# The product of the carried state with q, in a turned mLSTM chunk, on four quarters of the PE array in place of two

## The chip, the cores and the metric

The kernel runs on one core of a Trainium2 chip. The metric is the device time of one execution in microseconds (us); for a kernel it is the median of several executions. A profile of one further execution is read beside it. Engines are named as the profile names them: PE is TensorE's matmuls, PEld its weight loads, DVE is VectorE, ACT is ScalarE, POOL is GpSimd, SP issues the DMAs.

## The reference, cut to what matters

An mLSTM cell runs over 768 steps for 4 batches of 8 heads with 40 dimensions each; its output, seen as 3072 tokens of 320 values, goes through a feed-forward layer with a squared ReLU.

```python
def _attn_ref(q, k, v, i_gate, f_gate, o_gate):          # q, k, v, o_gate: (4, 8, 768, 40)
    ...
    for t in range(S):
        ...                                              # f_stab, i_stab: gates, stabilised
        C = f_stab[:, :, None, None] * C + i_stab[:, :, None, None] * np.einsum('bhd,bhe->bhde', vt, kt)
        n = f_stab[:, :, None] * n + i_stab[:, :, None] * kt
        h_tilde = np.einsum('bhde,bhe->bhd', C, qt)
        nq = np.einsum('bhd,bhd->bh', n, qt)[:, :, None]
        denom = np.maximum(np.abs(nq), 1.0)
        o = 1.0 / (1.0 + np.exp(-o_gate[:, :, t]))
        y[:, :, t] = o * h_tilde / denom
    return y

def _moe_ref(x, w_in, w_out):                            # x: (3072, 320); w_in: (320, 2048)
    h = np.maximum(x @ w_in, 0.0)
    return h * h @ w_out
```

The kernel does not step through time. It cuts the sequence into chunks of 128 steps: 4 batches of 6 chunks, s = 0 to 23, with c = s mod 6 the place in the batch. Within a chunk the output is a masked product (q k), weighted, times v; what came before the chunk enters as q times the state C that the chunk before left. At c = 0 there is no such state. C carries n as its 41st column, so a head gives 41 numbers for each step: 40 of the numerator and the denominator.

## The kernel before: the parts concerned

Chunks 0 to 5 take an older path. From chunk 6 on a chunk is "turned": its numerator stands with the 41 values of a head on partitions and the 128 steps along the row. With W = 512, P = 128, PR = 4, DP = 64, D = 40, D1 = 41:

```python
    ps_at = ctx.enter_context(tc.tile_pool(name="ps_at", bufs=3, space=PSUM))      # three PSUM banks
    ...
    def scores(s, o=(False, False)):              # L420: k q of a chunk, two banks of the pool
        d = st[s]
        sc = [bank(o[i]) for i in range(2)]       # bank(): ps_at.tile([P, W], F32, name="tp", tag="at")
        for j in range(PR):
            for i in range(2):
                rows = slice(DP * i, DP * i + D)
                nc.tensor.matmul(
                    sc[i][:, j, :], lhsT=d["kT"][rows, j, :], rhs=d["qT"][rows, j, :], start=True, stop=True,
                )
        d["sc"] = sc

    def weighted(s, spare=False):                 # L433: VectorE reads the two banks, writes P[0], P[1]
        ...
        for i in range(2):
            ...
            nc.vector.tensor_tensor(t, d["sc"][i], d["W"][:, heads, :], op=ALU.mult)

    def attend_turned(s):
        b, c = divmod(s, NB)
        d = st[s]
        halves = [slice(DP * i, DP * (i + 1)) for i in range(2)]
        live = [slice(DP * i, DP * i + D) for i in range(2)]
        numT = ps_at.tile([P, PR, P], F32, name="numT", tag="at")

        if c > 0:
            C = C_b[(s - 1) % 2]
            for j in range(PR):
                for i in range(2):                # L503: 40 rows and 64 columns of the array each
                    nc.tensor.matmul(
                        numT[halves[i], j, :], lhsT=C[live[i], j * D1 : j * D1 + DP], rhs=d["eA"][live[i], j, :],
                        start=(j == 0), stop=False, skip_group_check=True,
                    )
        for j in range(PR):
            for i in range(2):                    # L510: 128 rows, 64 columns
                h = PR * i + j
                nc.tensor.matmul(
                    numT[halves[i], j, :], lhsT=va_w[s % NKQ][:, h * D1 : h * D1 + DP],
                    rhs=d["P"][h % 2][:, h // 2, :] if s < KQ_SQ else d["P"][i][:, j, :],
                    start=(c == 0 and j == 0), stop=True, skip_group_check=True,
                )
        if c + 1 < NB:
            dC = ps_at.tile([P, PR, D1], F32, name="dC", tag="at")
            ...                                   # L520: eight matmuls, 128 rows, 40 columns: k v of the chunk

        tn = attn.tile([P, P // SQ, PR, SQ], F32, name="tn", bufs=1)
        nc.vector.transpose(tn[:].rearrange("p m j r -> p j m r"), numT[:].rearrange("p j t -> p (j t)"))   # L525
        d["tn"] = tn
        if c + 1 < NB:
            ...                                   # L531: the new C from dC and the decayed old one
```

The eight heads lie as h = 4 i + j: i picks the half of the array's rows in which a head's 40 dimensions of q and C stand (partitions 0 to 39 or 64 to 103). Before the change the same i also picks the half of the columns, and so of numT's partitions. `tn` goes out to DRAM and comes back with steps on partitions (N); `normalise_turned` divides by the denominator and multiplies by the output gate.

The order of work: a chunk takes four slots, each holding one part of the feed-forward of earlier tokens. Slot 0 is `score` (scores and weighted), then a part; slot 1 is `attend_turned`, then a part, and so on. A part is made of full-array matmuls: L625 and L636 (x w_in), L719 (h w_out, in seven products).

```python
        if at == 0:
            do(score, s)
        if at == 1:
            do(attend_turned, s)
            do(decays, s + 1)
            do(mask, s + 1)
            ...
        if which == 1:
            ffn1_main(g, i)
            ...
        elif g == 0:
            ffn2(g, *divmod(i, 2))
        else:
            ffn2_fast(g, i)
        if at == 2:
            ...
            do(normalise_turned, s)
```

Of the kernel before, what the change touches and what calls it, by code (L numbers as in the profile page):

```python
# [9 lines left out]
F32 = mybir.dt.float32  # L10
# [7 lines left out]
P = 128  # L18
# [11 lines left out]
def kernel(  # L30
# [27 lines left out]
    nc = tc.nc  # L58
    B, H, S, D = q.shape
# [3 lines left out]
    PR = H // 2  # L63
    DP = 64
    D1 = D + 1
    DM = H * D
# [5 lines left out]
    W = 4 * P  # L72
# [9 lines left out]
    ps_at = ctx.enter_context(tc.tile_pool(name="ps_at", bufs=3, space=PSUM))  # L82
# [16 lines left out]
    NKQ = 4  # L99
    kq_b = [consts.tile([P, 2, H, DP], F32, name=f"kq{i}") for i in range(NKQ)]  # L100

    va_w = [consts.tile([P, H * D1 + 24], F32, name=f"va{i}") for i in range(NKQ)]
# [177 lines left out]
    KQ_SQ, X_SQ = 7, 6  # L280
# [209 lines left out]

    def attend_turned(s):

        b, c = divmod(s, NB)
        d = st[s]
        halves = [slice(DP * i, DP * (i + 1)) for i in range(2)]
        live = [slice(DP * i, DP * i + D) for i in range(2)]
        numT = ps_at.tile([P, PR, P], F32, name="numT", tag="at")

        if c > 0:
            C = C_b[(s - 1) % 2]  # L500
            for j in range(PR):
                for i in range(2):
                    nc.tensor.matmul(  # L503
                        numT[halves[i], j, :], lhsT=C[live[i], j * D1 : j * D1 + DP], rhs=d["eA"][live[i], j, :],
                        start=(j == 0), stop=False, skip_group_check=True,
                    )
        for j in range(PR):
            for i in range(2):
                h = PR * i + j
                nc.tensor.matmul(  # L510
                    numT[halves[i], j, :], lhsT=va_w[s % NKQ][:, h * D1 : h * D1 + DP],
                    rhs=d["P"][h % 2][:, h // 2, :] if s < KQ_SQ else d["P"][i][:, j, :],
                    start=(c == 0 and j == 0), stop=True, skip_group_check=True,
                )
        if c + 1 < NB:
            dC = ps_at.tile([P, PR, D1], F32, name="dC", tag="at")
            for j in range(PR):
# [3 lines that stand above are left out]
                        dC[live[i], j, :], lhsT=d["kq"][:, 0, h, :D], rhs=d["vw"][:, h, :], start=True, stop=True,  # L521
                    )

        tn = attn.tile([P, P // SQ, PR, SQ], F32, name="tn", bufs=1)
        nc.vector.transpose(tn[:].rearrange("p m j r -> p j m r"), numT[:].rearrange("p j t -> p (j t)"))  # L525
        d["tn"] = tn
        if c + 1 < NB:
            Cn = C_b[s % 2][:, : PR * D1].rearrange("p (j d) -> p j d", d=D1)
            for rows in live:
                if c > 0:  # L530
                    nc.vector.tensor_tensor(Cn[rows], dC[rows], d["Cd"][rows], op=ALU.add)  # L531
                else:
                    nc.vector.tensor_copy(Cn[rows], dC[rows])
# [13 lines left out]
    def normalise_turned(s):  # L547
        d = st[s]
        N = d["N"].rearrange("p (g e j r) -> p g e j r", g=2, e=2, r=SQ)
        R = D - SQ  # L550
        den = N[:, :, 1, :, R]
        dm = work.tile([P, H], F32, name="dm")
        dm2 = dm[:].rearrange("p (g j) -> p g j", g=2)
        nc.vector.tensor_scalar(dm2, den, scalar1=-1.0, scalar2=1.0, op0=ALU.mult, op1=ALU.max)
        nc.vector.tensor_tensor(dm2, dm2, den, op=ALU.max)
        nc.vector.reciprocal(dm[:], dm[:])
        x = d["x"] = work.tile([P, 3 * P], F32, name="x_sb")
        x3 = x[:, :DM].rearrange("p (h d) -> p h d", d=D)
        x4, og = x[:, :DM].rearrange("p (g j d) -> p g j d", g=2, d=D), d["og"].rearrange("p (g j) d -> p g j d", g=2)
        nc.vector.tensor_tensor(x4[:, :, :, :SQ], N[:, :, 0], og[:, :, :, :SQ], op=ALU.mult)  # L560
        nc.vector.tensor_tensor(x4[:, :, :, SQ:], N[:, :, 1, :, :R], og[:, :, :, SQ:], op=ALU.mult)
        nc.vector.tensor_tensor(x3, x3, dm[:].unsqueeze(2).to_broadcast([P, H, D]), op=ALU.mult)
        nc.vector.tensor_copy(x[:, DM:], x[:, DM - KR : DM])
# [290 lines left out]
    for u in range(8):  # L854
        s = 2 + u // 2
# [72 lines left out]
    for n, (which, g, i) in enumerate(parts):  # L928
        s, at = 6 + n // 4, n % 4
# [5 lines left out]
# [4 lines that stand above are left out]
            if n > 4:  # L939
                do(turn_kq, s + 1)  # L940
            do(decay_C, s + 1)
            if s > X_SQ:
                do(turn_squares, s - 1)
            do(store_num, s)
            do(load, s + 4)
            if 8 <= s < 20:
                load_o(s + 4)
            do(load_num, s)
            do(pair_up, s + 3)
# [37 lines left out]
        if at == 2:  # L987
            do(lambda s: weigh(s, masked=True), s + 1)
            if n < 4:
                do(turn_kq, s + 1)  # L990
                do(scale_q, s + 1)
            do(normalise_turned, s)
            do(store_rows, s)
            do(load_squares, s + 2)
            do(load_rows, s)
            do(load_A, s + 2)
# [33 lines left out]
```

## Time and profile before

| what | value |
|---|---|
| median of 3 executions | 533.74 us (531.35 to 535.14) |
| span of the profiled execution | 534.1 us |
| mean granted PE clock | 0.986 |
| L503, q C | x240 matmul records, mean 275 ns |
| L510, P v | x288, mean 279 ns |
| L525, transpose of numT | x18, mean 717 ns |

In the profile each fp32 matmul of the program shows as two records of PE and two of PEld: the 8 matmuls of L503 in a chunk are 16 records, and 15 chunks with c > 0 make the 240. A record's duration is not the time that the matmul costs: records overlap, so the cost of a group is read from where it starts and where the next group starts. In a line of a timeline the columns are start in us, length in us, engine, line, operation, output and inputs, shape, and the number of records merged; a bracket tells of idle time before it. The shape `40*64` of a matmul is rows times columns of the array in use, `40x128` the moving operand.

### The profile page before, as it was taken

The page shows a single profiled execution, that of the slowest core. Times are in us where ns is not written, and L with a number is a line of the kernel's source. Part 1 is how long each engine was busy: PE and PEld are TensorE (multiplying, and loading weights), DVE is VectorE, ACT ScalarE, POOL GpSimd, SP SyncE. Part 2 cuts the span into 40 slices and gives each one's busy share as a digit, 9 for nine tenths or more (in the row PEclk, how much of TensorE's full clock was granted, in tenths as well). Part 3 has the DMA queues.
Part 4 walks back from the last instruction along what each step waited for, and adds up shares of the span by engine and source line. Part 5 has one row for each costly group of instructions (what it writes and reads, how often), then busy time and mean ns, then how long its engine had stood idle before and what let it go on. Part 6 is the DMA issues. An engine that isn't in the chain of part 4 may idle for free.

```text
span 534.1 us, 10320 instructions
## 1 busy us (share of the span) xinstructions
PE 523.7 (98%) x3928; PEld 457.7 (86%) x3929; DVE 328.5 (62%) x620; ACT 194.6 (36%) x460; POOL 91.4 (17%) x110
## 2 busy tenths in 40 slices
PE   8999989998999999999999999999999999999997
PEld 4878878886798898898898898898898898998997
DVE  8488988958874764654764754664764764532531
ACT  3766577552441422522422623313632413102100
POOL 3255633331320210110210200100210200000000
PEclk9897999998999999999999999999999999999999
DMA  9998699877576587585686576677566162110000
GB/s 193 224 197 179 162 159 203 193 180 157 109 155 116 119 161 139 116 168 116 134 170 130 114 153 111 154 150 135 131 137 127 55 128 49 53 42 2 26 25 26
DMA packets 239394, 68.06 MB, mean 127 GB/s; under 512 B 185744, under 2 KB 233872, under 8 KB 239344
## 3 DMA queue, kind: packets, MB, share of 16 engines
q1 hardware_dynamic: 239248, 67.20, 60.2%
q8 instruction: 31, 0.51, 0.4%
q10 hardware_dynamic: 96, 0.20, 0.1%
q14 instruction: 19, 0.16, 0.1%
HBM read 55.08 MB, written 17.86 MB: 137 GB/s over the span
## 4 chain that ended last, share of the span: by engine, by line
PE 85%; DVE 6%; ACT 3%; DMA 3%; SPq 2%; issue 1%; POOL 0%; DVEq 0%; POOLq 0%; ACTq 0%
PE h_ps L719 32%; PE h_ps L625 27%; PE h_ps L636 7%; PE tp L420 4%; PE numT L510 3%; PE h_ps L665 3%; PE numT L503 3%; PE hp L456 1%; DVE g L658 1%; DMA num_rows<-tn 1%; ACT W_sb L382 1%; SPq L308 1%; PE tp L408 1%; PE dC L520 1%; DMA kq<-in_q_dram 1%
## 5 line engine op out<-in xcount | busy, mean ns | idle before, releaser
L625 PE MATMUL h_ps<-xT,w_in 128*128 128x256 f32 x768 | 175.1, 384 | 0.6 <-ACT xT L610 0.6
L625 PEld LDWEIGHTS h_ps<-xT,w_in 128*128 128x128 f32 x768 | 143.8, 191 | 22.0 <-issue 1.2
L658 DVE TENSOR_TENSOR g<-r_sb 128x512 f32<-128x512 f32 x96 | 61.7, 701 | 67.0 <-ACT r_sb L651 67.0
L651 ACT ACTIVATE r_sb<-h_ps 128x512 f32<-128x512 f32 x96 | 49.9, 600 | 115.8 <-PE h_ps L636 112.7
L719 PE MATMUL h_ps<-w_out,g 128*128 128x160 f32 x528 | 77.0, 302 | 0.0
L719 PEld LDWEIGHTS h_ps<-w_out,g 128*128 128x128 f32 x528 | 72.5, 190 | 1.4
L358 POOL TENSOR_SCALAR_AFFINE_SELECT A_bc<-A_bc 128x1024 f32<-128x1024 f32 x22 | 26.2, 1192 | 216.8 <-ACT kq L368 183.0
L382 ACT ACTIVATE W_sb<-A_bc,b_T 128x128 f32<-128x128 f32 x176 | 53.8, 391 | 13.4 <-POOL A_bc L358 13.3
L719 PE MATMUL h_ps<-T,S 128*128 128x160 f32 x352 | 52.3, 302 | 0.0
L719 PEld LDWEIGHTS h_ps<-T,S 128*128 128x128 f32 x352 | 48.8, 190 | 3.0 <-ACT r_sb L651 3.0
L368 ACT ACTIVATE kq<-A_bc 64x512 f32<-64x512 f32 x30 | 18.8, 628 | 83.3 <-DMA A_bc<-a_rows 83.1
L636 PE MATMUL h_ps<-xT,w_in 64*128 64x256 f32 x384 | 49.0, 391 | 0.0
L636 PEld LDWEIGHTS h_ps<-xT,w_in 64*128 64x128 f32 x384 | 34.8, 186 | 12.3 <-issue 9.0
L525 DVE STREAM_TRANSPOSE tn<-numT 128x512 f32<-128x512 f32 x18 | 12.9, 717 | 36.2 <-PE numT L510 36.1
L433 DVE TENSOR_TENSOR P_sb<-tp,W_sb 128x512 f32<-128x512 f32 x46 | 29.5, 682 | 4.4 <-PE tp L420 4.4
L735 DVE TENSOR_TENSOR y_sb<-y_sb,h_ps 128x160 f32<-128x160 f32 x44 | 14.1, 320 | 26.4 <-PE h_ps L719 25.8
L394 POOL TENSOR_TENSOR vw<-va,W_sb 128x328 f32<-128x328 f32 x20 | 18.3, 916 | 67.4 <-ACT W_sb L382 60.6
L739 ACT COPY y_sb<-h_ps 128x160 f32<-128x160 f32 x11 | 3.2, 293 | 66.3 <-PE h_ps L719 66.3
L420 PEld LDWEIGHTS tp<-kqT 40*128 40x128 f32 x384 | 24.2, 187 | 3.3 <-issue 2.3
L420 PE MATMUL tp<-kqT 40*128 40x128 f32 x384 | 26.9, 279 | 0.0
L719 PE MATMUL h_ps<-T,g 128*128 128x160 f32 x176 | 25.7, 299 | 0.0
L719 PE MATMUL h_ps<-w_out,S 128*128 128x160 f32 x176 | 25.7, 299 | 0.0
(119 smaller groups left out, 610.6 us busy)
## 6 DMA issues: line engine op xcount, KB each, us to landing
A_bc<-a_rows SPq DMA_DIRECT2D x23, 512.0 KB, 5.0
raw<-in_moe_w_out_dram SPq DMA_DIRECT2D x16, 320.0 KB, 3.4
num_rows<-tn SPq DMA_DIRECT2D x18, 256.0 KB, 3.0
kq<-num_rows SPq DMA_DIRECT2D x72, 64.0 KB, 2.5
kqT<-kq_rows SPq DMA_DIRECT2D x34, 128.0 KB, 3.3
raw<-in_moe_w_in_dram SPq DMA_DIRECT2D x8, 512.0 KB, 4.7
kq<-in_k_dram SPq DMA_DIRECT2D x24, 160.0 KB, 4.4
va<-in_v_dram SPq DMA_DIRECT2D x24, 160.0 KB, 4.6
```

Of the source, the lines that this page charges most:

```text
L358: nc.gpsimd.affine_select(A[:], A[:], compare_op=ALU.is_ge, fill=-1e30, base=0, pattern=[[0, H], [1, P]], channel_multiplier=-1,)
L368: nc.scalar.activation(e[rows], st[s]["A"][0][rows, PR * i : PR * (i + 1), :], AF.Exp)
L382: nc.scalar.activation(d["W"][:, i * n + h, :], A[i][:, h, :], AF.Exp, bias=b_T[:, b, c, i * n + h : i * n + h + 1],)
L394: nc.gpsimd.tensor_tensor(d["vw"][:], d["va"][:], d["W"][:, :, P - 1 : P].to_broadcast([P, H, D1]), op=ALU.mult,)
L420: nc.tensor.matmul(sc[i][:, j, :], lhsT=d["kT"][rows, j, :], rhs=d["qT"][rows, j, :], start=True, stop=True,)
L433: nc.vector.tensor_tensor(t, d["sc"][i], d["W"][:, heads, :], op=ALU.mult)
L503: nc.tensor.matmul(numT[halves[i], j, :], lhsT=C[live[i], j * D1 : j * D1 + DP], rhs=d["eA"][live[i], j, :], start=(j == 0), stop=False, s ...
L625: nc.tensor.matmul(hs[i][:, n, :], lhsT=w_in[:, a, fb * P : (fb + 1) * P], rhs=xT[:, :, a, :], start=(n == 0 and a == 0), stop=False,)
L636: nc.tensor.matmul(hs[i][:, n, :], lhsT=w_in2[rows, 2 * pp + n, :], rhs=xT[rows, :, 2, :], start=False, stop=(n == 1),)
L651: nc.scalar.activation(rs[-1][:], h[:], AF.Relu)
L658: nc.vector.tensor_tensor(g4[:, :, i, :], r[:], r[:], op=ALU.mult)
L719: nc.tensor.matmul(to, lhsT=lhsT[:, p], rhs=rhs[:, p, :], start=(start and p == 0), stop=(p == NPAIR - 1), skip_group_check=True,)
```

## The change

The q C product of four pairs of heads used two quarters of the array: rows 0 to 63 with columns 0 to 63, and rows 64 to 127 with columns 64 to 127. The other two quarters stood empty. The change sends half of the heads to those. A head's row half is given by where its q and C lie, so it stays i; its column half becomes g, the parity of j. Heads with i = 0 and i = 1 would then meet in the same partitions of PSUM, so each i gets a bank of its own: `numT` becomes two banks, each half filled (two heads' width, e = 0 and 1, of four). The P v product follows the new places, and runs through bank 0 first and then bank 1. The transpose becomes two of half the width, and the normalisation reads the heads in their new order.

```diff
-        numT = ps_at.tile([P, PR, P], F32, name="numT", tag="at")
+        numT = [ps_at.tile([P, W], F32, name="numT", tag="at")[:].rearrange("p (c t) -> p c t", t=P) for _ in range(2)]
 
         if c > 0:
             C = C_b[(s - 1) % 2]
-            for j in range(PR):
-                for i in range(2):
+            for e in range(2):
+                for i, g in ((0, 0), (1, 1), (0, 1), (1, 0)):
+                    j = 2 * e + g
                     nc.tensor.matmul(
-                        numT[halves[i], j, :], lhsT=C[live[i], j * D1 : j * D1 + DP], rhs=d["eA"][live[i], j, :],
-                        start=(j == 0), stop=False, skip_group_check=True,
+                        numT[i][halves[g], e, :], lhsT=C[live[i], j * D1 : j * D1 + DP], rhs=d["eA"][live[i], j, :],
+                        start=(e == 0), stop=False, skip_group_check=True,
                     )
-        for j in range(PR):
-            for i in range(2):
-                h = PR * i + j
-                nc.tensor.matmul(
-                    numT[halves[i], j, :], lhsT=va_w[s % NKQ][:, h * D1 : h * D1 + DP],
-                    rhs=d["P"][h % 2][:, h // 2, :] if s < KQ_SQ else d["P"][i][:, j, :],
-                    start=(c == 0 and j == 0), stop=True, skip_group_check=True,
-                )
+        for i in range(2):
+            for e in range(2):
+                for g in range(2):
+                    j = 2 * e + g
+                    h = PR * i + j
+                    nc.tensor.matmul(
+                        numT[i][halves[g], e, :], lhsT=va_w[s % NKQ][:, h * D1 : h * D1 + DP],
+                        rhs=d["P"][h % 2][:, h // 2, :] if s < KQ_SQ else d["P"][i][:, j, :],
+                        start=(c == 0 and e == 0), stop=True, skip_group_check=True,
+                    )
...
-        nc.vector.transpose(tn[:].rearrange("p m j r -> p j m r"), numT[:].rearrange("p j t -> p (j t)"))
+        to = tn[:].rearrange("p m c r -> p c m r")
+        for i in range(2):
+            nc.vector.transpose(to[:, 2 * i : 2 * i + 2], numT[i][:, :2, :].rearrange("p c t -> p (c t)"))
...
-        dm2 = dm[:].rearrange("p (g j) -> p g j", g=2)
+        dm2 = dm[:].rearrange("p (j g) -> p g j", g=2)
...
-        x4, og = x[:, :DM].rearrange("p (g j d) -> p g j d", g=2, d=D), d["og"].rearrange("p (g j) d -> p g j d", g=2)
+        x4, og = x[:, :DM].rearrange("p (j g d) -> p g j d", g=2, d=D), d["og"].rearrange("p (j g) d -> p g j d", g=2)
```

## The prediction

> **What bounds the kernel now.** I read the page's shares first, then the chain that ended last, then the groups of PE by shape, and last the timeline of single chunks. The shares and the chain say which engine's time counts:
>
> ```profile
> PE 523.7 (98%) x3928; PEld 457.7 (86%) x3929; DVE 328.5 (62%) x620; ACT 194.6 (36%) x460; POOL 91.4 (17%) x110
> ...
> PE 85%; DVE 6%; ACT 3%; DMA 3%; SPq 2%; issue 1%; POOL 0%; DVEq 0%; POOLq 0%; ACTq 0%
> ```
>
> PE carries 85% of the chain and is never idle for long. A busy share of 98% alone would prove little, since matmul records overlap. So I asked who PE waited for from 132 us to the end, the stretch that holds the chunks 8 to 23: no wait of PE was listed there at all. In that stretch a nanosecond less between PE's starts is a nanosecond off the end, as long as no other engine takes over, and DVE (62% over the span) has room.
>
> What q C costs is read from starts. These are chunks 9 and 10 in the timeline of PE, the first with the scores before it:
>
> ```profile
> 166.96 1.06 PE L420 MATMUL tp<-kqT 40*128 40x128 f32 x16
> 167.95 3.72 PE L625 MATMUL h_ps<-xT,w_in 128*128 128x256 f32 x16
> 171.60 1.09 PE L503 MATMUL numT<-kq,C 40*64 40x128 f32 x16
> 172.62 1.09 PE L510 MATMUL numT<-P_sb,va 128*64 128x128 f32 x16
> 173.55 0.48 PE L520 MATMUL dC<-vw,kq 128*40 128x41 f32 x16
> ```
>
> ```profile
> 191.89 1.09 PE L503 MATMUL numT<-kq,C 40*64 40x128 f32 x16
> ...
> 192.91 1.09 PE L510 MATMUL numT<-P_sb,va 128*64 128x128 f32 x16
> ```
>
> From L503's first start to L510's it is 1.02 us in both (172.62 - 171.60, 192.91 - 191.89). How that is spent shows when the window on the tile is opened step by step from 191.88 us; the count after PE is how many matmul records touch the window:
>
> ```profile
> 191.88:191.90 0.02, 0.01 (x2) 0.02 (x2) 0.00 (x0) 1.00 0.54 83
> 191.88:192.04 0.16, 0.15 (x2) 0.16 (x4) 0.00 (x0) 1.00 0.72 115
> 191.88:192.06 0.18, 0.17 (x4) 0.18 (x6) 0.00 (x0) 1.00 0.71 114
> 191.88:192.15 0.27, 0.26 (x4) 0.27 (x6) 0.00 (x0) 1.00 0.66 104
> 191.88:192.17 0.29, 0.28 (x6) 0.29 (x8) 0.00 (x0) 1.00 0.65 103
> 191.88:192.26 0.38, 0.37 (x6) 0.38 (x8) 0.00 (x0) 1.00 0.63 99
> 191.88:192.28 0.40, 0.39 (x8) 0.40 (x10) 0.00 (x0) 1.00 0.62 99
> ```
>
> Starts come in pairs: two by 191.90, two more by 192.06, then by 192.17, by 192.28. The single records stand at 191.886 and 191.893, 192.046 and 192.053, 192.155 and 192.162, and so on: 7 ns within a pair, 109 ns from pair to pair, 160 ns for the first. One of a pair is in each quarter in use. Sixteen records are eight rounds: 0.160 + 6 x 0.109 + 0.206 = 1.02 us, where 0.206 is from the last pair to L510's first start, about 0.1 of it beyond a round.
>
> **What the Trainium skill says.** "TensorE: Matmul & The Clock Gate", section "Part 3: Packing small matmuls", lets row and column tiles compose and gives a span of one matmul plus about 4 ns for each further tile, with 10.6 times measured for 16 tiles. This trace agrees as far as it goes: 7 ns between two quarters. The same section's "The mechanism" says that a weight load overlaps matmuls in flight only where the row group differs, and that matmuls start in program order. Taken literally, that would forbid quarters 0/0 and 0/1 (row half/column half) to overlap. The trace disagrees: L510 uses all rows and differs in columns alone, and its 16 records take 0.93 us to L520's start (173.55 - 172.62), the same pairs. Nor is the start in program order: of the two records that one fp32 matmul makes, the second waits 109 ns for its quarter, while the next matmul in the other quarter has started. "TensorEngine Tiling (Array Packing)", section "Restrictions and Gotchas", says that different row tiles must not be in one PSUM bank at once. It is the reason for the second bank; no run here shows what would happen otherwise.
>
> **The change part by part.** *q C.* The eight matmuls of a chunk now fall on four quarters, two each, so each quarter has four records in place of eight. If a round holds four starts, 16 records are four rounds: 0.160 + 2 x 0.109 + 0.206 = 0.584 us, plus about 0.014 because a round's last start is 21 ns after its first and not 7. That is 0.60 in place of 1.02, so 0.42 to 0.44 us less in a chunk. Issue keeps up: L520, with 40 columns and 41 moving elements, puts 16 records in 0.40 us (173.55 to the next group's 173.95 in the same timeline, the drain included), under 25 ns a record, and four in 109 ns need 27.
>
> *How many chunks.* 15 have c > 0: 7 to 11, 13 to 17, 19 to 23. In chunk 7 PE waits for DVE's P anyway:
>
> ```profile
> 126.15 1.09 PE L503 MATMUL numT<-kq,C 40*64 40x128 f32 x16
> 129.04 0.43 PE L510 MATMUL numT<-P_sb,va 128*64 128x128 f32 x2 [1.80 <-DVE P_sb L433]
> 129.64 0.98 PE L510 MATMUL numT<-P_sb,va 128*64 128x128 f32 x13 [0.16 <-DVE P_sb L433]
> ```
>
> There q C lies wholly in the wait, and I count nothing for it. So 14 x 0.43 = 6.0 us.
>
> *P v.* Same eight matmuls, two column halves still in step, eight rounds. The halves now share P[0] in the first four matmuls and P[1] in the last four, so the second of DVE's products is needed 0.44 us later. Cost 0.
>
> *The banks.* The pool of three banks served four tiles of a chunk (two for the scores, numT, dC); now five. In the ring each tile takes the bank of the third before it: bank 0 of numT takes that of the last chunk's dC, as numT did; bank 1 takes that of the first score tile, and dC that of the second. So q C's second matmul now waits until DVE has made P[0]. In chunk 9 DVE's two products stand at
>
> ```profile
> 169.34 1.28 DVE L433 TENSOR_TENSOR P_sb<-tp,W_sb 128x512 f32<-128x512 f32 x2
> 173.77 0.72 DVE L525 STREAM_TRANSPOSE tn<-numT 128x512 f32<-128x512 f32 x1 [3.15 <-PE numT L510]
> ```
>
> so P[0] is ready near 170.0 and q C starts at 171.60: 1.6 us to spare. This is the shorter kind of gap: a slot-0 part of x w_in takes 3.65 us of PE, one of h w_out 4.54. Only in chunk 7 is it tight: there q C moves behind P[0] (DVE's first product ends near 128.99). From there: 0.44 of q C, the turn to L510 0.1 to 0.15, eight rounds 0.87: dC could begin near 130.5 against 130.35 before. Before, dC ran there with its halves out of step (L510's last record begins at 130.45, after dC's first) and the next part began at 131.28; in step it would begin near 131.0. Between 0.3 lost and 0.3 won: 0.
>
> *DVE.* One transpose of 512 elements (717 ns) becomes two of 256. From the other transposes, 538 ns for 384 and 1240 for 1024, an element is 1.1 ns and the fixed part 0.12 us, so I estimate 0.44 us each, 0.16 us more a chunk, 2.8 us over 18 chunks. None of it is on the path: DVE stood idle for 3.15 us before this transpose, and the first half can begin while PE still fills bank 1, so `tn` is done 0.28 us earlier after L510's end than before (0.44 in place of 0.72). The normalisation's operands only change strides, not lengths.
>
> *Sum.* 533.74 - 6.0 = 527.7 us.
>
> **The rivals.** (1) Quarters that share rows, or share columns, do not run at once, and only diagonal pairs do. Then four pairs of matmuls give eight rounds as before, and the time stays at 533.7. For it: no group of this kernel uses four quarters. Against it: L510 shows the shared-row pair and L420 (two row halves, all columns, 16 records in 0.99 us from 166.96 to 167.95) the shared-column pair, and four quarters ask for no more operand rows or output columns in a round than these. (2) PE looks ahead only over a few instructions, so a third and fourth quarter start late, after the second records of the first two. Rounds of 2, 4, 4, 4, 2: five in place of eight or four, a gain of 0.33 a chunk, 4.6 us, 529.1. For it: chunk 7, where a matmul blocked for P[1] also held back the next one for the free half. Against it: what is blocked there is a wait on a semaphore; once free, dC ran four records ahead of L510's last one. (3) The longer ring makes a wait: PE held for P[0] in many chunks. With 1.6 us to spare it would need DVE to be late by that much; 1 us in half of the chunks would cost 7 us and end at about 535. (4) The gain arrives on PE but another engine takes it: nothing stands near enough; DVE has 62%, and its longest wait is for PE.
>
> **Range and chances.** I give full concurrency 80%, the partial one 12%, none or a wait the rest. The three executions before span 3.8 us, so a median may be off by 1 us either way. From 526.0 to 530.5 should hold it 8 times in 10. Two per cent would be 10.7 us, which is more than the 14.3 us of L503's whole 14 chunks could plausibly yield; and a loss of that size needs the third rival in every chunk. Faster by over 2%: 0.03; within 2%: 0.95; slower: 0.02.
>
> **What would show it.** L503's first start to L510's: 0.58 to 0.61 us in the chunks from 8 on (1.02 if the first rival holds, 0.69 with the second). Stepwise windows with four starts in a round. L510 to L520 unchanged at 0.93. No new wait of PE for DVE's P after 132 us. Two transposes near 0.44 us, DVE's busy time up by about 3 us. The prediction is wrong if the 0.43 is there and the span does not follow, which would mean a wait I did not see, or if a round of four takes clearly more than 0.11 us.

## The result and the profile after

The changed kernel takes 527.16 us (median of 4 executions, 526.32 to 527.36) against 534.44 us of the kernel before (4 executions, 531.35 to 535.47). The ratio is 0.987, with a 95% interval of 0.983 to 0.991. The forecast was 527.7 us, taken from the median of three executions then known (533.74 us); a fourth has moved it to 534.44.

The shares and the chain of the page after, in the same two views as before:

```profile
PE 515.1 (98%) x3929; PEld 449.8 (86%) x3929; DVE 331.8 (63%) x638; ACT 194.2 (37%) x460; POOL 88.2 (17%) x110
...
PE 87%; DVE 5%; ACT 3%; DMA 2%; SPq 2%; issue 1%; POOL 0%; ACTq 0%; DVEq 0%; POOLq 0%
...
L534 DVE STREAM_TRANSPOSE tn<-numT 128x256 f32<-128x256 f32 x36 | 15.7, 447 | 23.2 <-PE numT L517 23.2
```

PE is as full as before and still carries the chain: the kernel is bound by the same thing and has less of it. The two transposes take 0.45 us each; over all chunks the records make 36 x 0.447 less 18 x 0.717 = 3.2 us more. DVE's busy time is up by 3.3 us (331.8 less 328.5), but it is a poor measure of so little: in a second profile of the kernel before it was 330.2.

Lines have moved by a few: q C is L508 now, P v L517, dC L527. This is chunk 9 in the timeline of PE:

```profile
168.24 0.67 PE L508 MATMUL numT<-kq,C 40*64 40x128 f32 x16
168.84 1.09 PE L517 MATMUL numT<-P_sb,va 128*64 128x128 f32 x16
169.76 0.48 PE L527 MATMUL dC<-vw,kq 128*40 128x41 f32 x16
```

From q C's first start to P v's it is 0.60 us (168.84 - 168.24), where it was 1.02. P v to dC is as before (0.924 us in chunk 10 of both profiles). The stepwise window on the tile, for chunk 10, shows how; its columns are the window, its length, then busy time and records of PE, of PEld and of DVE, the granted clock, the DMA share and GB/s:

```profile
188.10:188.13 0.03, 0.03 (x4) 0.03 (x4) 0.00 (x0) 1.00 0.51 81
188.10:188.25 0.15, 0.15 (x4) 0.15 (x8) 0.00 (x0) 1.00 0.70 117
188.10:188.29 0.19, 0.19 (x8) 0.19 (x12) 0.00 (x0) 1.00 0.75 124
188.10:188.36 0.26, 0.26 (x8) 0.26 (x12) 0.00 (x0) 1.00 0.79 129
188.10:188.40 0.30, 0.30 (x12) 0.30 (x16) 0.00 (x0) 1.00 0.77 124
188.10:188.47 0.37, 0.37 (x12) 0.37 (x16) 0.00 (x0) 1.00 0.73 116
188.10:188.51 0.41, 0.41 (x16) 0.41 (x16) 0.00 (x0) 1.00 0.67 107
```

The count of matmul records goes 4, 8, 12, 16 where it went 2, 4, 6, 8. The first four, which the program names for four different quarters, stand at 188.103, 188.110, 188.117 and 188.123: 6 to 7 ns apart. The next rounds begin at 188.263, 188.373 and 188.482, the 160, 110 and 109 ns of before. A round of four is no longer than a round of two.

The sum over all chunks is read from two points that lie far apart and have PE busy in between: chunk 8's q C and chunk 23's P v. Before, then after, in the timeline of PE:

```profile
151.33 1.09 PE L503 MATMUL numT<-kq,C 40*64 40x128 f32 x16
...
453.86 0.33 PE L510 MATMUL numT<-P_sb,va 128*64 128x128 f32 x2
```

```profile
148.39 0.67 PE L508 MATMUL numT<-kq,C 40*64 40x128 f32 x16
...
445.00 0.55 PE L517 MATMUL numT<-P_sb,va 128*64 128x128 f32 x6
```

That is 302.53 us and 296.61: 5.92 us less, 14 chunks at 0.423. From chunk 23's P v to PE's last start it is 76.79 us in both. But the two profiled spans differ by 8.9 us (534.1 and 525.2) and the medians by 7.3. So 2.9 us of the spans lie before chunk 8's q C (151.33 and 148.39), where the change touches only chunks 6 and 7. One part of it shows in the windows of PE behind chunk 7, before and then after; the columns are the window, its length, PE busy (records), granted clock, DMA share and GB/s:

```profile
126.90:130.30 3.40, 1.44 (x22) 1.00 0.75 127
130.30:133.70 3.40, 3.40 (x27) 0.53 0.58 179
```

```profile
126.90:130.30 3.40, 2.58 (x49) 1.00 0.73 174
130.30:133.70 3.40, 3.40 (x14) 1.00 0.62 147
```

In the profile before, PE waited for DVE in chunk 7, and then ran for some 3.4 us at half clock. The 48 matmul records that follow (L665) took 14.4 us from the first start to the next group's; in the profile after they took 13.1. Whether that half-clock stretch belongs to the change was the open question. It decides between a change worth 5.9 us and one worth 7 or more.

### The profile page after: what moved, and what is told of

It reads as the page before. It is cut to its first block, busy times and chain, and to the rows that moved or that the text cites. A ratio compares the mean times of both kernels' runs of the same rounds, so it can differ in the third digit from the quotient of the medians.

```text
span 525.2 us, 10338 instructions
## 1 busy us (share of the span) xinstructions
PE 515.1 (98%) x3929; PEld 449.8 (86%) x3929; DVE 331.8 (63%) x638; ACT 194.2 (37%) x460; POOL 88.2 (17%) x110
## 4 chain that ended last, share of the span: by engine, by line
PE 87%; DVE 5%; ACT 3%; DMA 2%; SPq 2%; issue 1%; POOL 0%; ACTq 0%; DVEq 0%; POOLq 0%
PE h_ps L728 33%; PE h_ps L634 27%; PE h_ps L645 7%; PE tp L420 4%; PE numT L517 3%; PE h_ps L674 2%; PE hp L456 2%; PE numT L508 2%; PE idle L787 1%; DVE g L667 1%; PE tp L408 1%; SPq L308 1%; DMA num_rows<-tn 1%; PE A_ps L349 1%; PE dC L527 1%
## 5 line engine op out<-in xcount | busy, mean ns | idle before, releaser
L358 POOL TENSOR_SCALAR_AFFINE_SELECT A_bc<-A_bc 128x1024 f32<-128x1024 f32 x22 | 24.3, 1103 | 214.2 <-ACT kq L368 155.4
L382 ACT ACTIVATE W_sb<-A_bc,b_T 128x128 f32<-128x128 f32 x176 | 53.8, 390 | 13.3 <-POOL A_bc L358 13.1
L534 DVE STREAM_TRANSPOSE tn<-numT 128x256 f32<-128x256 f32 x36 | 15.7, 447 | 23.2 <-PE numT L517 23.2
```

Source lines behind the costliest of these rows:

```text
L358: nc.gpsimd.affine_select(A[:], A[:], compare_op=ALU.is_ge, fill=-1e30, base=0, pattern=[[0, H], [1, P]], channel_multiplier=-1,)
L382: nc.scalar.activation(d["W"][:, i * n + h, :], A[i][:, h, :], AF.Exp, bias=b_T[:, b, c, i * n + h : i * n + h + 1],)
```

## The experiments

**The changed kernel and the kernel before, once more.** Both are unaltered.

> The changed kernel once more, unaltered, for a second profile and a narrower ratio. Theory: the change is worth 14 x 0.423 = 5.9 us on PE (ratio 0.989), and what the first pair of profiles shows beyond that (8.9 us of span) are two stretches of half clock near 14 and 130 us that only the kernel before had in its profile; in other executions they come and go, so the medians should differ by 6 to 7.5 us and this profile's span should lie at 525 to 528. Rival: the change itself is worth 7.3 us or more, by something beyond q C: then the span is 525 again, and no half-clock stretch stands near 130 us in any profile of it, while the kernel before always has one.

Measured: 527.34 us (6 executions), ratio 0.9885, interval 0.985 to 0.992, span 523.6. Chunk 8's q C to chunk 23's P v is again 296.61. There is no half clock near 130 us.

> The kernel before the change, unaltered, for a second profile. Theory (the half-clock stretch behind the wait in chunk 7 depends on how the idle time falls into the clock's windows): it may or may not be there; the 14 chunks from 8 on take 1.02 us each for q C whether or not. Rival (it belongs to the kernel before): it is there again between 125 and 135 us.

Measured: one execution, 533.97 us, span 532.2. The same windows of PE in this profile:

```profile
126.90:130.30 3.40, 1.40 (x23) 1.00 0.74 156
130.30:133.70 3.40, 3.40 (x27) 1.00 0.50 150
```

PE was about as idle as in the first profile of this kernel, and no half clock followed. Chunk 8 to chunk 23 is 302.53 as before. So the stretch does not come in every execution of the kernel before, and further below it comes in kernels with four quarters too (the runs with ScalarE's work moved and with q C twice).

**The banks without the quarters.** The kernel before, with numT in two banks and the transpose in two, and q C left in its two quarters:

```diff
-        numT = ps_at.tile([P, PR, P], F32, name="numT", tag="at")
+        numT = [ps_at.tile([P, W], F32, name="numT", tag="at")[:].rearrange("p (c t) -> p c t", t=P) for _ in range(2)]
...
-                        numT[halves[i], j, :], lhsT=C[live[i], j * D1 : j * D1 + DP], rhs=d["eA"][live[i], j, :],
-                        start=(j == 0), stop=False, skip_group_check=True,
+                        numT[j // 2][halves[i], j % 2, :], lhsT=C[live[i], j * D1 : j * D1 + DP], rhs=d["eA"][live[i], j, :],
+                        start=(j % 2 == 0), stop=False, skip_group_check=True,
...
```

> The new layout of banks without the new quarters: numT in two banks (heads j = 0, 1 in the first, 2, 3 in the second), five tiles in the ring of three, two transposes of 256; q C stays in two quarters. Theory (all of the gain is in the quarters): q C to P v stays 1.02 us, transposes take 0.45 us each, DVE is busy some 3 us more, and the time is that of the kernel before within 1 us (533 to 535). Rival (the banks, or the earlier transposes, give part of the gain): 532.5 or less. Rival (the longer ring costs something that the quarters pay for): above 536.

Measured: 533.72 us (22 executions), ratio to the kernel before 0.9992, interval 0.997 to 1.001. Chunk 10 in the timeline:

```profile
192.59 1.09 PE L503 MATMUL numT<-kq,C 40*64 40x128 f32 x16
...
193.61 1.09 PE L510 MATMUL numT<-P_sb,va 128*64 128x128 f32 x16
194.31 0.89 DVE L527 STREAM_TRANSPOSE tn<-numT 128x256 f32<-128x256 f32 x2 [1.24 <-PE numT L510]
```

q C to P v is 1.02, the transposes are two and earlier, the ring has its five tiles, and nothing is won or lost that the interval shows. From chunk 8's q C to chunk 23's P v it is 302.53 us, as in the kernel before. All of the gain is in the quarters, and in that stretch the second bank and the second transpose cost nothing. (DVE is busy 329.3 us here, 0.8 more than in the first profile of the kernel before and not the 3 expected.) After 132 us PE waits for no other engine, here or in the changed kernel, so the rival of a new wait in the ring falls for these chunks. In chunk 7 the wait is there, as forecast: q C itself now stands behind P[0], 3.2 us in this profile and 2.6 in the changed kernel's.

**The order in which the quarters are named.**

```diff
-            for e in range(2):
-                for i, g in ((0, 0), (1, 1), (0, 1), (1, 0)):
+            for i, g in ((0, 0), (1, 1), (0, 1), (1, 0)):
+                for e in range(2):
```

> The changed kernel, but the program names both matmuls of one quarter one after the other before it goes to the next quarter. Theory A (each quarter has a queue of its own, and PE hands out at least 16 weight loads and matmuls ahead): four starts in a round as before, q C to P v 0.60 us, time as the changed kernel's. Theory B (a quarter takes only two matmul records, one running and one waiting, before the hand-out stops): the second quarter starts one or two rounds late, six or seven rounds, 0.82 to 0.93 us, time 3 to 4.6 us above the changed kernel's. Theory C (strictly in program order): no overlap of quarters but at the seams, over 1.02 us, over 6 us above.

Measured: 529.12 us (8 executions), ratio 0.9926, interval 0.990 to 0.995. The stepwise window on the tile in chunk 10:

```profile
187.74:187.75 0.01, 0.01 (x1) 0.01 (x1) 0.00 (x0) 1.00 0.68 115
187.74:187.79 0.05, 0.05 (x4) 0.05 (x4) 0.00 (x0) 1.00 0.95 159
187.74:187.91 0.17, 0.17 (x5) 0.17 (x9) 0.00 (x0) 1.00 0.94 150
187.74:187.95 0.21, 0.21 (x8) 0.21 (x12) 0.00 (x0) 1.00 0.86 137
```

Still four in a round. The starts are now 13 ns apart in place of 7, at 187.743, .756, .769 and .783, and q C to P v is 0.617 us. The records do not name their quarter; but two of one quarter never stood under 109 ns apart in the groups of before with 128 moving elements, so these four lie in four. Theory A holds: PE had twelve matmul records of the first three quarters ahead of the fourth quarter's first, and that one started 40 ns after the first of all. Chunk 8 to chunk 23 is 296.89, 0.28 us over the changed kernel's. The median is 1.8 us over it. The intervals of the two ratios overlap, and q C accounts for 0.3 of it; five of these eight executions had a mean granted clock under 0.993, and one of the six of the changed kernel's second series.

**q C twice.** The products of q C are done twice over in each chunk, so that the carried part counts double.

```diff
-            for e in range(2):
+            for twice, e in ((0, 0), (0, 1), (1, 0), (1, 1)):
                 for i, g in ((0, 0), (1, 1), (0, 1), (1, 0)):
...
-                        start=(e == 0), stop=False, skip_group_check=True,
+                        start=(e == 0 and twice == 0), stop=False, skip_group_check=True,
```

> The changed kernel with q C done twice in each chunk (the carried part counts double in the output). Theory: four more rounds of four starts, 0.436 us a chunk and 14 or 15 chunks: q C to P v 1.03 us, the time 6.1 to 6.5 us above the changed kernel's, and so near the kernel before. Rival (a round of four is held up once the run of it is longer, by weight loads that fall behind): over 0.5 us a chunk, over 7 us.

Measured: 536.15 us (14 executions), ratio 1.0009, interval 0.999 to 1.003. By the medians that is 8.8 us over the changed kernel, which speaks for the rival; by the ratios to the kernel before (1.0009 and 0.9885) it is 6.6, and the profile does not speak for it either. q C to P v is 1.034 us in the chunks from 8 on, 0.436 more for four rounds more. Chunk 8 to chunk 23 is 302.73, 6.11 over 296.61 = 14 x 0.436. Rounds of four go on at the same pace in a run of eight. The rest lies before chunk 8, in a PE wait of 3.3 us in chunk 7 and a half-clock stretch behind it.

**The wait in chunk 7.** In every profile of the unaltered kernels PE waits there, 1.6 to 2.6 us, and then the clock may or may not fall. I tried to take the wait away, to measure the change without it. In the code `n` counts the slots from chunk 6 on, so that chunk 7's slots 0 and 1 are n = 4 and 5. First a part of the feed-forward (slot 1's) was put ahead of chunk 7's numerator; `part` is a function made of the lines that ran it in place:

```diff
+        if n == 5:
+            part(which, g, i)
         if at == 1:
             do(attend_turned, s)
...
+        if n != 5:
+            part(which, g, i)
```

> The changed kernel with one part of the feed-forward moved ahead of chunk 7's numerator, so that PE has 4.6 us of work while DVE makes P. Theory: the wait of 2.6 us for P in chunk 7 goes, nothing else moves to the path, and with no idle stretch there the clock has no cause to fall: 2.6 to 4 us less than the changed kernel, about 524. Rival: chunk 7's own results come 2 us later and PE waits for them, or for DVE, in chunk 8 or at the x w_in part after it: same time as the changed kernel.

Measured: 527.23 us (6 executions), ratio 0.988, as the changed kernel. The timeline of PE has the wait in another place:

```profile
119.91 8.34 PE L674 MATMUL h_ps<-w_out,g 128*128 128x320 f32 x30
129.49 0.81 PE L674 MATMUL h_ps<-w_out,g 128*128 128x320 f32 x2 [1.23 <-POOL w_out L215]
```

The part that came earlier needed the last piece of w_out, which was not ready. The rival was right about the time, though it had looked for the wait elsewhere: it moved to that piece.

Second, what holds P? In the profile of the changed kernel ScalarE stands 5.75 us on the DMA of that last piece, before the relu; behind the relu stand four squares on DVE, behind them P. So ScalarE's work on the piece was put behind the relu, in the changed kernel and in the one before:

```diff
-                self.words()
+                if len(self.b) != len(pieces) - 2:
+                    self.words()
```

> The changed kernel, with ScalarE's work on the last piece of w_out put behind the relu of the part before it, so that ScalarE no longer stands 5.75 us on that piece's DMA while relu, squares, P and then q C of chunk 7 wait in a row behind it. Theory (that DMA is the root of PE's wait in chunk 7): the wait of 1.6 to 2.6 us goes or falls below 0.5, the clock has no idle stretch there, and the time is 1.5 to 2.6 us below the changed kernel's, 524.8 to 526. Rival (as in the run with the part moved ahead, the last piece then comes too late and PE waits for it): no change.

> The same move of ScalarE's work in the kernel before the change, q C in two quarters. It takes away PE's wait in chunk 7, and with it the half-clock stretch that the kernel before had behind that wait. Then chunk 7's q C is on the path too, and the change is worth 15 x 0.423 = 6.3 us: theory, this run less the same move in the changed kernel is 6 to 7 us. Rival (the change is worth over 7 us by something else than q C): the difference is over 7.5 us.

Measured: 527.85 us (5 executions) in the changed kernel, 533.27 (22) in the other. The relu came at 119.14 in place of 123.84, and PE still waited 2.2 us for P. My theory fell. The timeline of DVE in the changed kernel with this move shows why:

```profile
122.31 0.32 DVE L206 TENSOR_SCALAR mag<-mag 128x320 f32<-128x320 f32 x1
122.66 0.87 DVE L210 TENSOR_SCALAR mag<-mag 128x320 int32<-128x320 int32 x1
123.56 0.49 DVE L211 SCALAR_TENSOR_TENSOR mag<-raw,mag 128x320 int32<-128x320 int32 x1
123.97 3.16 DVE L668 TENSOR_TENSOR g<-r_sb 128x512 f32<-128x512 f32 x4
127.16 1.29 DVE L434 TENSOR_TENSOR P_sb<-tp,W_sb 128x512 f32<-128x512 f32 x2
```

DVE has no gap here: it works off a row in which P stands last, and the squares take 3.16 us of it. The DMA was not the root. In this changed kernel the clock fell as well:

```profile
126.90:130.30 3.40, 2.39 (x30) 0.70 0.69 134
130.30:133.70 3.40, 3.40 (x29) 0.80 0.64 182
```

The premise of the pair, no wait, was not met, so its difference (5.4 us by the medians, 0.9852 and 0.9966 by the ratios) decides nothing about 6 or 7.

Third, the four squares behind P, in the changed kernel and in the one before; they belong to a part that is used much later:

```diff
             do(score, s)
+            if n == 4:
+                square_half()
+                square_half()
...
                     relu_half()
-                    square_half()
+                    if n != 3:
+                        square_half()
```

> The changed kernel, with the four squares of the part before chunk 7 put behind P of chunk 7 in VectorE's order. Theory (P stands behind those squares, and the squares behind ScalarE's late relu; it is VectorE's order that holds PE): PE's wait for P in chunk 7 goes, the stretch from chunk 6's P v to chunk 8's q C falls to 42 to 43 us (43.5 to 48.7 in the profiles so far), no half clock stands near 130 us, and the time is 1.5 to 3 us below the changed kernel's, 524.5 to 526. Rival: PE then waits for the last piece of w_out or for something else there, as with the part moved ahead, and the time stays at 527.

> The same move in the kernel before the change. With PE never waiting in chunk 7, all 15 chunks with a carried state pay for q C: theory, the changed kernel with the move is 15 x 0.423 = 6.3 us below this one (5.8 to 6.9), and this one 1.5 to 3 us below the kernel before. Rival (something else in the change gives 1 us or more): over 7.3 us.

Measured: 524.07 us (4 executions, 523.64 to 524.95; ratio to the kernel before 0.9825, interval 0.980 to 0.985) in the changed kernel, and 530.09 us (6 executions, 529.72 to 530.72; ratio 0.9935, interval 0.991 to 0.996) in the one before. Chunk 7 of the first, on DVE and on PE:

```profile
122.92 1.29 DVE L433 TENSOR_TENSOR P_sb<-tp,W_sb 128x512 f32<-128x512 f32 x2
124.62 2.50 DVE L667 TENSOR_TENSOR g<-r_sb 128x512 f32<-128x512 f32 x4 [0.41 <-ACT r_sb L660]
```

```profile
120.24 4.57 PE L674 MATMUL h_ps<-w_out,g 128*128 128x320 f32 x16
124.75 0.67 PE L508 MATMUL numT<-kq,C 40*64 40x128 f32 x16
125.34 1.09 PE L517 MATMUL numT<-P_sb,va 128*64 128x128 f32 x16
```

P comes 4.05 us earlier than after the change alone (122.92 in place of 126.97), and PE goes through chunk 7 without a wait, with all four quarters at once. From chunk 6's P v to chunk 8's q C it is 42.02 us (42.44 in the kernel before with the same move), where the unaltered kernels had 44.0 to 46.5. Neither profile has half clock near 130 us. The executions of each lie within 1.3 us of one another; those of the kernel before, taken alongside, span 3.8 us (532.14 to 535.96). And the difference of the two, free of the wait, is 6.02 us; from the scatter of the ten executions I estimate it to 0.9 us either way. It lies within what 15 chunks were expected to give, and below the rival's 7.3. (15 x 0.423 would be 6.35; in the changed kernel's profile a weight load waited once, 0.4 us, for DVE.)

Last, both moves:

> The changed kernel with the squares behind P and ScalarE's work on the last piece of w_out behind the relu. Theory: with the squares out of P's way the other move has nothing left to give; PE's wait is gone in both, and the time is within 1 us of the run with the squares alone. Rival: the earlier relu lets VectorE and the banks of the next part go on sooner, 1 us or more less.

Measured: 524.43 us (4 executions, 524.08 to 527.05), ratio 0.984, interval 0.981 to 0.987. The second move adds nothing to the first. The changed kernel with the squares behind P is faster than both kernels of the comparison, and the best version run here.

## Why the prediction was right

*q C on four quarters.* Right in mechanism and size: 0.60 us from q C to P v was forecast and 0.598 measured, 0.423 us a chunk, 5.92 us over 14 chunks against the forecast 6.0. From chunk 8's q C to chunk 23's P v it is 302.53 us in all five profiles with two quarters and 296.61 to 296.99 in the seven with four and one q C; from there to PE's last start it is 76.79 in all. So the gain reaches the end whole, and what scatters lies before chunk 8. The first rival (diagonal pairs only) is refuted by the stepwise window, the second (a short look-ahead) also by the run in another order. What the Trainium skill says in "TensorE: Matmul & The Clock Gate", "Part 3: Packing small matmuls", that row and column tiles compose at about 4 ns for each further tile, agrees but for the size: 6 to 7 ns here. Its words on matmuls that start in program order do not agree; the run in another order shows that most plainly.

*P v, banks, DVE.* Right: P v to dC is unchanged; no wait of PE for P after 132 us; two transposes of 0.45 us each (0.44 forecast), 3.2 us of transposes in all (2.8 forecast), and the run with the banks alone shows that they cost nothing after chunk 7. The working had slips that did no harm. 0.12 us and 1.1 ns an element would be 0.40 us for 256 elements; the 0.44 is what the whole transpose's 717 ns leave without the other 256. The dC records ahead of P v's last one in chunk 7 were three (130.35 to 130.45 us), not four. And that no run shows two row halves in one bank is not so: in the kernel before, the two q C records of a pair come from different row halves and write one bank 7 ns apart, in different partitions. What no run shows is four quarters writing one bank, and so whether the second bank was needed.

*Chunk 7.* Nothing was counted and nothing came. From the end of P[0] to the next part's start it is 1.98 us after (127.66 to 129.64) and also 1.98 in the second profile of the kernel before (128.68 to 130.66). But one reading of mine there was wrong in part: I put dC's slowness in the first profile down to its halves being out of step. They are out of step in the second profile of that kernel too, where the next part begins 0.51 us after P v's last record starts (130.15 to 130.66); in the first it is 0.83 (130.45 to 131.28). The difference is the half clock, which I had not looked for in the windows.

*The remainder.* The measured 7.3 us is 1.3 over the forecast, 0.7 of it by the fourth execution of the kernel before. In both pairs of unaltered profiles the spans differ by more than 5.92: by 8.9 and by 8.6 (532.2 and 523.6), with the rest before chunk 8. From chunk 6's P v to chunk 8's q C it is 46.5 and 45.2 us before, 45.0 and 44.0 after; without the 1.3 us of the 48 records and the 0.3 of dC at half clock, the 46.5 would be 44.9. Up to chunk 6's P v it is 104.8 and 104.2 us before, 103.4 and 102.7 after, though the two kernels do the same work there; the runs with the two banks and with the squares moved, whose q C is that of before, begin it at 103.3 and 103.7, the changed kernel with ScalarE's work moved at 103.9. So that stretch scatters by 1 us and more whatever q C does, and the difference free of the wait is 6.02.

The granted clock goes with the scatter. In the changed kernel's second series, executions with a mean clock of 0.993 or more average 526.7 us (5 of 6) and 532.8 in the kernel before (11 of 28 alongside), 6.1 apart; below that clock it is 529.7 (1) and 535.1 (17). Over all series whose clocks are known, 9 of 10 executions of the changed kernel reach that clock and 27 of 74 of the kernel before; the larger difference of the medians goes with that. That the quarters cause this is not shown: of the altered kernels with four quarters and the wait left in, 3 of 8, 3 of 6, 3 of 5 and 3 of 14 reach it, of those with two 11 of 22 and 16 of 22. I take about 6 us as the worth of the change; the rest stays open. The intervals (4.6 to 9.3 us by the first ratio, 4.4 to 7.9 by the second) do not prove it to a microsecond, and that the median came within 0.6 us of the forecast is in part luck.

## What to carry to other kernels

A matmul that uses at most half of the rows and half of the columns leaves three quarters of the array to others: look at the shape in the profile. Here each row half had a PSUM bank of its own; whether one bank would do was not run. What it is worth is read in starts, from the group's first to the next group's first, and not in busy time; on an engine that never waits in the stretch, that gain reaches the end nanosecond for nanosecond. Where medians differ by more than the stretch explains, compare two fixed points inside it in several profiles before looking for a second cause.

## What the runs showed of the hardware that I had not expected

- PE looks far ahead across quarters: in the other order a quarter's first matmul started 40 ns after the first of all, past twelve matmul records that the program names earlier. Each start was then 13 ns from the last, where it is 7 when consecutive matmuls lie in different quarters.
- Four quarters at once take the same 109 ns for a round as two, with 128 moving fp32 elements each.
- A half-clock stretch can follow a wait of PE, and one of 3.4 us cost 1.3 us here. Over nine profiles it followed waits in chunk 7 of 1.8, 2.2, 2.4, 3.2 and 3.3 us, and not waits of 1.6, 2.1, 2.3 and 2.6. So the length of the wait does not decide. Where it falls does, as far as these profiles go. In the first profile of the kernel before, half clock begins at 14.46, 41.77 and 130.51 us: 8 and 26 times 3.413 us apart. In the other profiles too, stretches begin whole multiples of 3.413 us from one another, and last one, two or three of them. So each profile has a grid of such windows, and the one that holds most of the wait can be found. Here it is with the next one, in the two profiles of the kernel before:

```profile
127.10:130.51 3.41, 1.45 (x24) 1.00 0.77 141
130.51:133.92 3.41, 3.41 (x24) 0.50 0.57 169
...
127.18:130.59 3.41, 1.69 (x32) 1.00 0.74 172
130.59:134.00 3.41, 3.41 (x18) 1.00 0.51 144
```

PE is idle for 1.96 us of the one and for 1.72 of the other. In the nine profiles:

| kernel | wait (us) | window | idle in it (us) | half clock from its end |
|---|---|---|---|---|
| q C twice | 3.3 | 126.44 to 129.85 | 2.47 | yes |
| two banks | 3.2 | 124.36 to 127.77 | 2.44 | yes |
| ScalarE's work moved, four quarters | 2.2 | 124.87 to 128.28 | 2.24 | yes |
| ScalarE's work moved, two quarters | 2.4 | 126.07 to 129.48 | 2.15 | yes |
| before, first profile | 1.8 | 127.10 to 130.51 | 1.96 | yes |
| before, second profile | 2.1 | 127.18 to 130.59 | 1.72 | no |
| other order | 2.3 | 125.64 to 129.06 | 1.66 | no |
| changed, second profile | 1.6 | 124.56 to 127.97 | 1.52 | no |
| changed, first profile | 2.6 | 126.27 to 129.69 | 1.45 | no |

The longest wait without half clock, 2.6 us, lies across two windows, 1.15 and 1.45 us in each. This ordering is read from chunk 7 alone, and idle time is not the whole rule: near 66 us, in other work, a window of the second profile of the kernel before with 1.68 us idle was followed by half clock. The Trainium skill's "TensorE: Matmul & The Clock Gate", "Part 1: The HAM clock gate", has a free-running window of 3413 ns, which agrees with the 3.413 us here. Its table lets the clock fall after an idle window; here 1.96 us of idle time in one were enough.
